# The last attention turn of an attention and token-mixer kernel: 18 tiles in place of 16, with the sums in two blocks

## Chip, cores and metric

The kernel runs on one core of a Trainium2 chip. The metric is device time in microseconds (us) for one execution, the median of several runs. A profile is one execution recorded by the hardware profiler; its times count from the first instruction. TensorE shows as PE in the profile (its weight loads as PEld), ScalarE as ACT, VectorE as DVE, GpSimd as POOL and SyncE as SP.

## What is computed

The reference runs two layers, each an attention and a mixer, both with a residual and a layer norm in front. There are 2,048 rows of 512 channels, 32 query heads of 16 channels, and one head of keys and values that all query heads share.

```python
def _A_ref(x, wq, wk, wv, wo):          # B, S, D = 1, 2048, 512; H = 32; Dh = 16
    q = (x @ wq).reshape(B, S, H, Dh).transpose(0, 2, 1, 3)
    k, v = x @ wk, x @ wv
    p = softmax(einsum("bhqd,bkd->bhqk", q, k) * Dh ** -0.5)
    o = einsum("bhqk,bkd->bhqd", p, v)
    return o.transpose(0, 2, 1, 3).reshape(B, S, H * Dh) @ wo
def _B_ref(x, w1, b1, w2, b2):          # mixes along the 2048 rows; F = 1792
    h = layernorm(x)
    u = gelu(einsum("bsd,sf->bdf", h, w1) + b1)
    return (einsum("bdf,fs->bds", u, w2) + b2).transpose(0, 2, 1)
x = x + _A_ref(layernorm(x), ...);  x = x + _B_ref(layernorm(x), ...)   # twice
```

## The kernel before, in words

**Tiles of attention.** Each layer's attention is cut into 32 groups, called cycles here: 4 blocks of 512 queries times 8 sets of 4 heads. A cycle has 32 tiles: 16 blocks of 128 keys times 2 pairs of heads. A layer has 1,024 tiles, counted by `scored` as they are begun. One tile passes through three engines:

- `scores` (line 915): two matmuls (line 921), one for each head of the pair, write 128 keys by 2 x 512 queries into a PSUM buffer called sc. There are three such buffers (`bank2`, lines 100 and 101, `bufs=3`), of two banks each, used in turn.
- ScalarE takes the exponential of the tile into an SBUF tile p (line 931). Either it reads PSUM itself, and the buffer is free when it ends, or the tile is *copied*: VectorE first copies sc into p (line 929), which frees the PSUM buffer, and ScalarE then works in place on p. In the profile the first kind is `p<-sc`, the second `p<-p`.
- `sums` (line 933): the matmuls of line 937 multiply p with the values and a column of ones, and add to the cycle's accumulator acc. The program issues two per tile; the trace holds four, each on 32 columns of the array, and those of one tile run side by side.

The tiles whose sums have not been issued are the list `pend`. `drain(count)` (line 942) issues the sums of the oldest ones. The p tiles come from a ring of 8 and a second ring of 4, of which every third tile takes one (`room`, line 908): twelve in all. The remaining two PSUM banks are single ones; cycles use them in turn for acc, and the bank that is not the current accumulator serves other products.

**Other work between the tiles.** When a pair of cycles is done, its sums are divided by the row sums on VectorE and multiplied with a part of the output weights: a *projection* (`project`, line 888; matmuls on line 898), into the spare single bank, whose result VectorE adds to x (`put`, line 903; the addition is on line 906). Mixer products that are known already are also placed between the tiles.

**Turns.** The order of all this is written by hand. `run` (line 997) asks `Mixer.turn` (line 1238) for the next turn, a tuple of numbers, and walks through it:

```python
if k > 0:                       # line 1041
    self.more(mix, k)           # begin k tiles; 10 + k: the last of the k is copied
elif k == 0:
    parts.pop(0)(self.spare())  # the next projection or half of a product
else:
    self.drain(-k)              # the sums of -k tiles; then a step of queued VectorE work
```

A turn is chosen when exactly `lag` tiles are pending. `lag` is 4 in the later part of a layer's attention and 2 in its last 16 tiles (line 1017). If the number differs, the turn is PLAIN, (2, -2), in which the number of sums is what brings the pending tiles back to `lag`, at most four. FOURS is the turn that is taken when more than three projections wait and 30 tiles of the last cycle are left to be summed. That is once in each layer, with 998 of 1,024 tiles begun (hence tile 998) and four pending. Its four projections belong to the second-to-last pair of cycles and have three matmuls each. Behind FOURS come plain turns to the end of the cycle. Then `rest` (line 1289) issues the sums of what is pending, and goes on with the mixer: its first product there is pu_e (line 1214).

**Around it.** Some 40 us ahead of the first FOURS another turn, QUAD (line 44), places four projections of six matmuls each and holds two blocks of six sums; the trace shows the second of them from 974.37 us.

Of the kernel before, what the change touches and what calls it, by code (L numbers as in the profile page):

```python
# [45 lines left out]
    2, -2, 13, 0, 13, -4, 13, 0, 13, -4, 3, -6, 13, 0, 13, 0, 3, -6, 13, -4, 3, -4,  # L46
)
ENTRY = (1, 0, 13, 0, 13, -4, 13, -4, 13, -4, 13, -4)
FOURS = (3, -4, 12, 0, 13, 0, -4, 3, -4, 12, 0, 13, -4, 0)
SHORT = (2, 0, 3, -4, 3, -4)  # L50
TINY = (2, 0, 2, -4)
PLAIN = (2, -2)
# [20 lines left out]
def kernel(  # L73
# [729 lines left out]
    class Attention:  # L803
# [193 lines left out]
        def run(self, mix, proj):  # L997
# [10 lines left out]
            while self.scored < total:  # L1008
# [31 lines left out]
                for k in turn:  # L1040
# [15 lines left out]
                    else:  # L1056
# [11 lines left out]
                        if self.pieces:  # L1068
                            self.pieces.pop(0)()
                        elif turn in (LONG, COPIED, ENTRY, DOUBLE, QUAD, QUAD_TO_FOUR, FOURS, WHOLE):  # L1070
                            room = 2.4 if turn in (COPIED, ENTRY, QUAD, QUAD_TO_FOUR) else 1.0
# [15 lines left out]
    class Mixer:  # L1087
# [150 lines left out]
        def turn(self, att):  # L1238
# [20 lines left out]
            if len(self.projections) > 3 and att.to_boundary() == 30 and att.scored > 2 * NKT * (NB * NG - 1):  # L1259
                return FOURS, [projection] * 4  # L1260
            if len(self.projections) > 1:
# [473 lines left out]
```

## Time and profile before

| | |
|---|---|
| median of 3 runs | 2511.52 us (2510.51 to 2512.19) |
| the profiled execution, its own time | 2511.45 us |
| its span, first to last instruction | 2509.7 us |
| mean granted TensorE clock | 0.998 |
| score matmuls, line 921 | 4,096, 683.4 us busy |
| sum matmuls, line 937 | 8,192, 999.7 us busy |
| exponentials from PSUM, line 931 | 1,441, 1404.4 us busy |
| exponentials of copied tiles, line 931 | 607, 659.4 us busy |
| copies by VectorE, line 929 | 607, 742.7 us busy |
| projection matmuls, line 898 | 360, 100.5 us busy |

A row of the timeline has the start, the length, the engine, the line of the kernel, the operation, the names of output and inputs, the shapes and how many instructions were merged into the row. In square brackets stands the idle time before it, and what ended it. Matmuls are pipelined: the next one starts before the last one's end, so a cost is read from start to next start. Rows of weight loads show idle time whenever a block of matmuls needs no new weights for a while; that alone is no wait of TensorE.

### The profile page before, as it was taken

What the parts mean: (1) busy time and instruction counts of PE and PEld (TensorE: products, weight loads), DVE (VectorE), ACT (ScalarE), POOL (GpSimd) and SP (SyncE); (2) the same over time, 40 slices, a digit from 0 to 9 for tenths busy, and PEclk for the clock granted to TensorE, in tenths of its full rate; (3) what the DMA queues carried; (4) which work ended last, traced back from release to release, by engine and by line L of the source; (5) the groups of instructions that cost most, each with busy time, mean ns of one, the idle gap of its engine ahead of it and who ended that gap; (6) DMA issues with size and microseconds to landing.
All of it is one profiled execution on the core that took longest, in us unless ns stands there. A gap on an engine that the chain in (4) does not pass through costs nothing. (4 is left out here: it accounts for less than half of the span.)

```text
span 2509.7 us, 41974 instructions
## 1 busy us (share of the span) xinstructions
PE 2493.1 (99%) x16170; PEld 1242.5 (50%) x16170; DVE 1554.8 (62%) x2462; ACT 2102.5 (84%) x2345; POOL 148.2 (6%) x235
## 2 busy tenths in 40 slices
PE   9999999999999999999999999999999999999999
PEld 6444344444444444588864343444444444445887
DVE  6565566667766776564445565666677667765522
ACT  6999999999999999653349999999999999995511
POOL 5000000000000000141000000000000000002200
PEclk9999999999999999999999999999999999999999
DMA  3221201111111111134414112111111111102343
GB/s 116 75 66 41 65 29 39 32 41 31 39 31 39 31 41 31 43 110 149 127 51 126 51 47 57 31 39 31 41 31 39 31 43 33 41 26 67 106 125 95
DMA packets 168679, 143.56 MB, mean 57 GB/s; under 512 B 17650, under 2 KB 132368, under 8 KB 167952
## 3 DMA queue, kind: packets, MB, share of 16 engines
q1 hardware_dynamic: 168464, 140.72, 18.9%
q8 instruction: 132, 2.16, 0.4%
q14 instruction: 83, 0.68, 0.1%
HBM read 97.67 MB, written 26.22 MB: 49 GB/s over the span
## 5 line engine op out<-in xcount | busy, mean ns | idle before, releaser
L931 ACT ACTIVATE p<-sc 128x1024 f32<-128x1024 f32 x1441 | 1404.4, 1050 | 63.5 <-PE sc L921 62.7
L929 DVE COPY p<-sc 128x1024 f32<-128x1024 f32 x607 | 742.7, 1224 | 525.2 <-PE sc L921 439.6
L937 PE MATMUL acc<-p,vaug 128*32 128x512 f32 x8192 | 999.7, 600 | 0.0
L921 PE MATMUL sc<-qs,kst 51*128 51x512 f32 x4096 | 683.4, 432 | 8.2 <-DVE kst L595 2.7
L931 ACT ACTIVATE p<-p 128x1024 f32<-128x1024 f32 x607 | 659.4, 1086 | 12.9 <-DVE p L929 8.2
L921 PEld LDWEIGHTS sc<-qs,kst 51*128 51x128 f32 x4096 | 338.8, 185 | 560.1 <-ACT p L931 390.2
L937 PEld LDWEIGHTS acc<-p,vaug 128*32 128x32 f32 x8192 | 218.6, 109 | 488.9 <-issue 474.6
L1467 PE MATMUL py<-u,w 128*128 128x512 f32 x1344 | 307.4, 390 | 0.0
L1467 PEld LDWEIGHTS py<-u,w 128*128 128x128 f32 x1344 | 251.9, 188 | 52.3
L1455 ACT CAST w<-w2r 128x896 fp32r<-128x896 f32 x64 | 60.3, 945 | 185.6 <-PE py L1467 177.8
L1214 PE MATMUL pu<-hb,w 128*128 128x512 f32 x792 | 209.6, 406 | 0.0
L1214 PEld LDWEIGHTS pu<-hb,w 128*128 128x128 f32 x792 | 140.9, 188 | 57.7 <-issue 31.8
L1201 POOL TENSOR_TENSOR w<-w1r,w 128x256 fp32r<-128x256 f32 x86 | 69.9, 821 | 1572.9 <-ACT w L1199 1571.8
L1456 DVE TENSOR_TENSOR w<-w2r,w 128x896 fp32r<-128x896 f32 x64 | 72.3, 1130 | 110.7 <-ACT w L1455 110.7
L857 DVE RECIPROCAL o<-o 128x128 f32<-128x128 f32 x120 | 113.3, 944 | 8.8 <-DMA o<-ev 8.8
L898 PE MATMUL po<-wo,hl 128*128 128x512 f32 x360 | 100.5, 412 | 0.1
L418 PE MATMUL pq<-hT,wq 128*128 128x512 f32 x312 | 81.4, 404 | 0.0
L898 PEld LDWEIGHTS po<-wo,hl 128*128 128x128 f32 x360 | 62.6, 188 | 34.0 <-issue 16.4
L839 DVE COPY ev<-acc 128x512 f32<-128x512 f32 x64 | 43.6, 682 | 56.0 <-PE acc L937 56.0
L1214 PE MATMUL pu_l<-hb,w 128*128 128x512 f32 x336 | 77.1, 389 | 0.0
L1473 DVE SCALAR_TENSOR_TENSOR x<-py,b2c,x 128x512 f32<-128x512 f32 x32 | 24.0, 750 | 81.6 <-PE py L1467 81.6
L1199 ACT CAST w<-w1r 128x256 fp32r<-128x256 f32 x86 | 34.3, 406 | 47.3 <-PE pu_l L1214 12.7
(191 smaller groups left out, 1181.9 us busy)
## 6 DMA issues: line engine op xcount, KB each, us to landing
w1r<-in_B_w_dram SPq DMA_DIRECT2D x224, 128.0 KB
w2r<-in_B_w_dram SPq DMA_DIRECT2D x64, 448.0 KB
qs<-qd SPq DMA_DIRECT2D x384, 64.0 KB
qd<-q SPq DMA_DIRECT2D x64, 256.0 KB
o<-ev SPq DMA_DIRECT2D x128, 128.0 KB
x<-in_A_x_dram SPq DMA_DIRECT2D x16, 256.0 KB
hd<-hT SPq DMA_DIRECT2D x2, 2048.0 KB
out_dram<-x SPq DMA_DIRECT2D x16, 256.0 KB
```

Of the source, the lines that this page charges most:

```text
L418: yield nc.tensor.matmul(out, a, c, start=(k == 0), stop=(k == len(terms) - 1))
L857: nc.vector.reciprocal(o[:, 1, c], o[:, 1, c])
L898: nc.tensor.matmul(po, a, c, start=(k == 0), stop=(k == 3 * len(parts) - 1))
L921: nc.tensor.matmul(sc[:, j, :], kst[kt // 4][rows, kt % 4 * P : (kt % 4 + 1) * P], qs[i % NQ][rows, j0 // 2, :], start=True, stop=True,)
L929: nc.vector.tensor_copy(pt, sc)
L931: nc.scalar.activation(pt, sc, AF.Exp, scale=0.25)
L937: nc.tensor.matmul(self.acc[i][c : c + 32, :], vaug[:, kt].rearrange("p d k -> p (d k)"), pt[:, j, :], start=(kt == 0), stop=(kt == NKT - ...
L1201: eng.tensor_tensor(w[:, 1], raw, f32(w[:, 0]), op=ALU.subtract)
L1214: nc.tensor.matmul(pu, a, c, start=(start and k == 0), stop=(stop and k == 5))
L1455: nc.scalar.copy(w[:, 0], raw)
L1456: nc.vector.tensor_tensor(w[:, 1], raw, f32(w[:, 0]), op=ALU.subtract)
L1467: nc.tensor.matmul(py, a, d, start=(c == 0 and f == 0 and k == 0), stop=(c == 1 and f == NFH - 1 and k == 2),)
```

## The change

One tuple is replaced; nothing else in the file differs.

```diff
-FOURS = (3, -4, 12, 0, 13, 0, -4, 3, -4, 12, 0, 13, -4, 0)
+FOURS = (-2, 13, 0, 13, 0, 13, -6, -4, 13, 0, 13, 0, 13, -2, -6)
```

Read with the rules above, the old turn begins 3 tiles, sums 4, begins 2 (the second copied), runs a projection, begins 3 (the third copied), runs a projection, sums 4, begins 3, sums 4, begins 2 (copied), a projection, begins 3 (copied), sums 4, a projection. That is 16 tiles begun, four of them copied, 16 summed and four projections. It leaves four tiles pending at 1,014 begun, where `lag` is 2, so a plain turn of two tiles and four sums follows.

The new turn sums 2, then begins three groups of 3 tiles (the third of each copied) with a projection after the first and the second group, sums 6 and 4, which makes ten in a row, begins three such groups again with the other two projections, and sums 2 and 6, eight in a row. That is 18 tiles begun, six of them copied, 20 summed and the same four projections. It leaves two tiles pending at 1,016 begun, which is where the old turn and its plain turn end.

## Prediction

> **What bounds the kernel now.** I read the page first, then the busy time by stretch, then the timeline of TensorE and ScalarE around the changed turn.
>
> ```profile
> PE 2493.1 (99%) x16170; PEld 1242.5 (50%) x16170; DVE 1554.8 (62%) x2462; ACT 2102.5 (84%) x2345; POOL 148.2 (6%) x235
> ```
>
> TensorE looks full over the whole span, but its ends are modelled, so a share says little about one turn. The turn runs once per layer, near 1013 us and near 2259 us. By stretch (columns: length, then busy time and count of PE, PEld, DVE, ACT, POOL, the granted clock, DMA):
>
> ```profile
> 1013.10:1031.90 18.80, 18.75 (x132) 6.95 (x128) 8.28 (x12) 17.97 (x20) 0.00 (x0) 1.00 0.04 15
> 1031.90:1041.00 9.10, 9.10 (x60) 2.50 (x56) 0.00 (x0) 7.77 (x10) 0.67 (x1) 1.00 0.01 3
> 2259.40:2278.20 18.80, 18.75 (x132) 6.94 (x128) 8.31 (x12) 17.96 (x20) 0.00 (x0) 1.00 0.04 15
> ```
>
> The two layers are alike to 0.03 us, so one is worked out and doubled. In the 18.80 us both TensorE (18.75) and ScalarE (17.97) are nearly full: the turn is balanced between the two. VectorE (8.28) and the DMAs (0.04) have room. TensorE's rows, from the turn's first scores to the scores that follow it:
>
> ```profile
> 1013.14 0.96 PE L921 MATMUL sc<-qs,kst 51*128 51x512 f32 x6
> 1014.03 1.92 PE L937 MATMUL acc<-p,vaug 128*32 128x512 f32 x16
> 1015.88 0.73 PE L921 MATMUL sc<-qs,kst 51*128 51x512 f32 x4
> 1016.55 0.97 PE L898 MATMUL po<-wo,hl 128*128 128x512 f32 x3
> 1017.45 1.10 PE L921 MATMUL sc<-qs,kst 51*128 51x512 f32 x6
> 1018.60 0.96 PE L898 MATMUL po<-wo,hl 128*128 128x512 f32 x3
> 1019.49 1.92 PE L937 MATMUL acc<-p,vaug 128*32 128x512 f32 x16
> 1021.35 0.97 PE L921 MATMUL sc<-qs,kst 51*128 51x512 f32 x6
> 1022.25 1.92 PE L937 MATMUL acc<-p,vaug 128*32 128x512 f32 x16
> 1024.10 0.73 PE L921 MATMUL sc<-qs,kst 51*128 51x512 f32 x4
> 1024.76 0.97 PE L898 MATMUL po<-wo,hl 128*128 128x512 f32 x3
> 1025.66 1.07 PE L921 MATMUL sc<-qs,kst 51*128 51x512 f32 x6
> 1026.65 1.92 PE L937 MATMUL acc<-p,vaug 128*32 128x512 f32 x16
> 1028.51 0.97 PE L898 MATMUL po<-wo,hl 128*128 128x512 f32 x3
> 1029.40 0.74 PE L921 MATMUL sc<-qs,kst 51*128 51x512 f32 x4
> 1030.07 1.92 PE L937 MATMUL acc<-p,vaug 128*32 128x512 f32 x16
> 1031.93 0.73 PE L921 MATMUL sc<-qs,kst 51*128 51x512 f32 x4
> ```
>
> The rows are the tuple itself: scores of 3 tiles, sums of 4, scores of 2, a projection, and so on; the last two before 1031.93 are the plain turn (2, -2), which scores two tiles and here sums four because four were pending. So the stretch of 18 tiles and 20 sums is before's turn of 16 tiles plus one plain turn. From start to next start: three tiles of scores 0.89, two 0.67 (1015.88 to 1016.55), four sums 1.85, a projection 0.90. ScalarE over the same stretch:
>
> ```profile
> 1013.02 1.08 ACT L931 ACTIVATE p<-p 128x1024 f32<-128x1024 f32 x1
> 1013.97 3.79 ACT L931 ACTIVATE p<-sc 128x1024 f32<-128x1024 f32 x4
> 1017.99 1.06 ACT L931 ACTIVATE p<-p 128x1024 f32<-128x1024 f32 x1 [0.23 <-DVE p L929]
> 1018.95 1.92 ACT L931 ACTIVATE p<-sc 128x1024 f32<-128x1024 f32 x2
> 1020.76 1.06 ACT L931 ACTIVATE p<-p 128x1024 f32<-128x1024 f32 x1
> ...
> 1032.53 7.44 ACT L931 ACTIVATE p<-sc 128x1024 f32<-128x1024 f32 x8 [0.58 <-PE sc L921]
> ```
>
> An exponential from PSUM takes 0.91 of ScalarE (two from 1018.95 to 1020.76), one of a copied tile 0.95 (1013.02 to 1013.97). ScalarE runs almost without a break while sums come four at a time; the rows show 0.23 and 0.58 idle. The row that carries the end is the last: eight exponentials back to back, then this.
>
> ```profile
> 1039.10 0.14 PEld L937 LDWEIGHTS acc<-p,vaug 128*32 128x32 f32 x4 [0.77 <-ACT p L931]
> ...
> 1041.00 3.06 PE L1214 MATMUL pu_e<-hb,w 128*128 128x512 f32 x12
> ```
>
> After the stretch the last sums wait for ScalarE (0.77), and the mixer's rest follows them at once. So whatever delays the exponential of 1032.53 delays the layer's end by as much; nothing behind it absorbs that.
>
> **The change, part by part.** *Work.* Before: 16 tiles and 16 sums, then a plain turn's 2 tiles and 4 sums. After: 18 tiles and 20 sums, leaving the same two pending. Same scores, sums and projections, no DMA, no step moved past a queue (no queued division step is left: VectorE has only copies and additions here). Six tiles are copied by VectorE in place of four: two exponentials at 0.95 for 0.91, 0.08 us of ScalarE, and 2 x 1.22 on VectorE, which has room. What changes is the order: sums of 2, then three groups of 3 scores with 2 projections between, sums of 10, the same groups again, sums of 8.
>
> *TensorE alone.* Before by pieces: 4 x 0.89 + 3 x 0.67 scores, 5 x 1.85 sums, 4 x 0.90 projections: 18.42, against 18.79 in the rows (1013.14 to 1031.93), so 0.37 is waits. A block of six sums is in the trace some 40 us earlier, behind groups of two, three and three tiles with two projections, much as here; ScalarE beside it:
>
> ```profile
> 974.37 2.78 PE L937 MATMUL acc<-p,vaug 128*32 128x512 f32 x24
> 977.08 0.50 PE L921 MATMUL sc<-qs,kst 51*128 51x512 f32 x2
> ```
>
> ```profile
> 973.60 1.06 ACT L931 ACTIVATE p<-p 128x1024 f32<-128x1024 f32 x1
> 974.55 1.94 ACT L931 ACTIVATE p<-sc 128x1024 f32<-128x1024 f32 x2
> 976.35 1.07 ACT L931 ACTIVATE p<-p 128x1024 f32<-128x1024 f32 x1
> 977.71 1.02 ACT L931 ACTIVATE p<-sc 128x1024 f32<-128x1024 f32 x1 [0.28 <-PE sc L921]
> ```
>
> Six take 2.71, two more than four for 0.86: 0.43 a sum and 0.13 once per block. Ten then take 4.43, eight 3.57; no row has such blocks. The other end is a block that scales whole, 10 x 1.85 / 4 = 4.63 and 3.70; I take the first, which two rows give, and keep 0.33 a layer for the range. A two joined to the four ahead of it costs 0.86. After by pieces: 6 x 0.89 + 0.86 + 4.43 + 3.57 + 4 x 0.90 = 17.80. TensorE has 0.62 less to do per layer, from fewer, longer blocks.
>
> The Trainium skill, "TensorEngine Tiling (Array Packing)", section Key Properties, says that a change of tiling mode drains TensorE; by that rule fewer blocks are a gain. The rows agree so far as each block costs more than its tiles; its result is the rival of TensorE's work below.
>
> *ScalarE during a long block.* This is what I hold to decide. While TensorE sums, it makes no scores, and ScalarE lives on what lies ready: three PSUM buffers and a copied tile. The six-sum rows show it: sums begin at 974.37, ScalarE has work until 977.42, next scores start at 977.08 and their exponential at 977.71, 0.6 after. Six sums already cost 0.28 of idle ScalarE. Four more cost 4 x 0.43 = 1.7 on top.
>
> *The walk.* Zero is 1013.14, the end of the sums ahead; t0 is the first tile. Two rows give the releases:
>
> ```profile
> 1016.73 1.22 DVE L929 COPY p<-sc 128x1024 f32<-128x1024 f32 x1 [2.65 <-PE sc L921]
> 1017.87 0.68 DVE L906 TENSOR_TENSOR x<-x,po 128x512 f32<-128x512 f32 x1
> ```
>
> ```profile
> 1017.81 0.38 PEld L921 LDWEIGHTS sc<-qs,kst 51*128 51x128 f32 x4 [0.18 <-ACT p L931]
> ```
>
> Scores reuse a PSUM buffer three tiles on, 0.05 after its reader ends (1017.76 to 1017.81); a pair's copy starts 0.85 after the pair's scores (1015.88 to 1016.73) and takes 1.22.
> - Two sums first: scores of t0 at 0.86, exponential at 1.46. Before it was at 0.83 (1013.97): 0.63 lost.
> - Exponentials: t0 1.46, t1 2.37, t2 (copied) 3.28, t3 4.23, t4 5.14, t5 (copied) 6.05, t6 7.00, t7 7.91, t8 (copied) 8.82; ScalarE is free at 9.77.
> - Scores between: t0 to t2 at 0.86, projection 1.75, t3 at 2.65; t4 waits for t1's exponential (2.37 + 1.02) and starts at 3.44, t5 behind it; second projection 4.10; t6 after t3's exponential, 5.30; t7 after t4's, 6.21, t8 behind it. Each exponential finds its scores ready.
> - Sums of ten start at 6.21 + 0.67 = 6.88 and end at 11.31; exponential of t9 at 11.91. ScalarE idles 2.14.
> - Same again, 10.45 later: sums of eight start at 17.33, end at 20.90; the first of the last eight exponentials at 21.50.
>
> Before it stood at 19.39 (1032.53). The change costs 2.11 us a layer: ScalarE gains idle time of 0.63, 2.14 and about 1.3 and loses that of before. The first projection's addition starts when t2's copy ends (about 3.1) and takes 0.68: done at 3.8, before the second projection at 4.10. The last eight tiles run as before, shifted.
>
> *The sum.* 2 x 2.11 = 4.2 us on the profiled execution, 2511.45 (span 2509.7 and 1.75 around it), 0.07 under the median of 2511.52: 2515.6. If blocks scale whole: 2 x 0.33 more, 2516.3.
>
> **Rivals.**
> - *TensorE's work decides.* ScalarE's idle time turns out covered, and the turn falls to TensorE's pieces: 18.79 to 17.80, at most 0.99 a layer, 2509.5. For it: TensorE is busy 18.75 of 18.80. Against it: the 0.28 idle of a mere six sums. Even this is under 0.2% of gain, so nothing here can be faster by more.
> - *VectorE falls behind in the score groups.* Three copies and two additions are 3 x 1.22 + 2 x 0.68 = 5.0 us in the 6.0 of nine tiles. t5's copy ends at 3.44 + 0.85 + 1.22 = 5.51 and t8's scores need its buffer at 6.55, so it decides once a copy is over 1.0 us late. With both additions ahead of it, 1.36: 0.36 in four groups, 1.4 us, to 2517.0, slower by over 0.2%. Against it: program order puts one addition ahead of that copy, not two.
> - *The clock drops.* TensorE now waits for PSUM inside the score groups, 0.5 us or so at t4 and at t7. At half the clock the blocks of ten and eight would take 8.0 longer a layer, 16 in all: 2531.6. It decides if waits longer than those of before come. Against it: the stretch from 1031.90 holds waits of 0.77 at a granted 1.00.
>
> The Trainium skill, "TensorE: Matmul & The Clock Gate", section "A second HAM failure mode: psum-queue depth-cycling", tells of micro-idles between groups that made the clock swing; no run here shows that so far.
>
> **How the numbers follow.** 0.2%, about what a measurement of this kernel can tell from no change, is 5.0 us, from 2506.5 to 2516.5. Idle ScalarE 0.71, which lies within it (2515.6 to 2516.3); TensorE's work 0.05, within; VectorE 0.17 and the clock 0.04, slower; 0.03 for a gain that no row shows. So faster 0.03, same 0.76, slower 0.21. The range starts at 2513.8: the forecast less the opening's 0.63 in both layers and 0.3 a layer of backlog I may have missed. It ends at 2518.0: VectorE's case with blocks that scale whole. Outside lie TensorE's case, the clock's and the unseen gain, 0.12, and some of the rest.
>
> **What would show it.** In the profile after, both turns hold blocks of 40 and 32 sum matmuls, the first from about 6.9 us after 1013.14 and some 4.4 long; ScalarE shows idle gaps of about 2.1 and 1.3 us ended by scores; the row of eight exponentials starts at about 1034.6 in place of 1032.53, and 4.2 later than before in the second layer. VectorE's copies of scores number 4 more over the span. I am wrong if ScalarE stays busy through the ten sums, if the rows of eight start no later than before, or if the time moves elsewhere.

## Result and the profile after

| | before | after |
|---|---|---|
| median of 17 runs | 2512.64 us (2509.75 to 2513.82) | 2516.71 us (2514.22 to 2519.39) |
| span of the profiled execution | 2509.7 | 2515.0 |

The ratio is 1.0018, with a 95% interval from 1.0011 to 1.0024. The median is 4.1 us longer where 4.2 was forecast, 0.16% of the time and so within the 0.2% that was named as no change. (Of 17 runs the median of before is 1.1 us above that of the first three, and the forecast of 2515.6 misses the new median by as much. That 4.1 and 4.2 agree to 0.1 is therefore partly luck; what bears the forecast out is the two turns below.)

The profile after shows where the 4 us lie. TensorE's rows of the first layer's turn, as before from the timeline:

```profile
1012.15 2.78 PE L937 MATMUL acc<-p,vaug 128*32 128x512 f32 x24
1014.87 0.97 PE L921 MATMUL sc<-qs,kst 51*128 51x512 f32 x6
1015.76 0.96 PE L898 MATMUL po<-wo,hl 128*128 128x512 f32 x3
1016.66 0.51 PE L921 MATMUL sc<-qs,kst 51*128 51x512 f32 x2
1017.46 0.73 PE L921 MATMUL sc<-qs,kst 51*128 51x512 f32 x4 [0.30 <-ACT p L931]
1018.12 0.97 PE L898 MATMUL po<-wo,hl 128*128 128x512 f32 x3
1019.32 0.50 PE L921 MATMUL sc<-qs,kst 51*128 51x512 f32 x2 [0.23 <-ACT p L931]
1020.23 0.73 PE L921 MATMUL sc<-qs,kst 51*128 51x512 f32 x4 [0.41 <-ACT p L931]
1020.90 4.50 PE L937 MATMUL acc<-p,vaug 128*32 128x512 f32 x40
1025.33 0.96 PE L921 MATMUL sc<-qs,kst 51*128 51x512 f32 x6
...
1031.36 3.64 PE L937 MATMUL acc<-p,vaug 128*32 128x512 f32 x32
1034.93 0.74 PE L921 MATMUL sc<-qs,kst 51*128 51x512 f32 x4
```

The first row holds the four sums ahead of the turn and its two. The walk's zero, the end of the four, is 1012.15 + 1.85 = 1014.00 here. (This execution had reached the turn 0.87 us later than the one of before, which has nothing to do with the change.) Then come groups of scores that wait for ScalarE to free PSUM (0.30, 0.23, 0.41), and one row of 40 matmuls: the ten sums, 4.43 from start to next start. ScalarE, from the tile ahead of the turn to the row of eight:

```profile
1013.88 1.07 ACT L931 ACTIVATE p<-p 128x1024 f32<-128x1024 f32 x1
1015.47 1.94 ACT L931 ACTIVATE p<-sc 128x1024 f32<-128x1024 f32 x2 [0.51 <-PE sc L921]
1017.29 1.06 ACT L931 ACTIVATE p<-p 128x1024 f32<-128x1024 f32 x1
1018.24 1.94 ACT L931 ACTIVATE p<-sc 128x1024 f32<-128x1024 f32 x2
1020.05 1.08 ACT L931 ACTIVATE p<-p 128x1024 f32<-128x1024 f32 x1
1021.00 1.96 ACT L931 ACTIVATE p<-sc 128x1024 f32<-128x1024 f32 x2
1022.80 1.09 ACT L931 ACTIVATE p<-p 128x1024 f32<-128x1024 f32 x1
1025.93 1.94 ACT L931 ACTIVATE p<-sc 128x1024 f32<-128x1024 f32 x2 [2.03 <-PE sc L921]
...
1033.27 1.10 ACT L931 ACTIVATE p<-p 128x1024 f32<-128x1024 f32 x1
1035.54 7.54 ACT L931 ACTIVATE p<-sc 128x1024 f32<-128x1024 f32 x8 [1.18 <-PE sc L921]
```

Three gaps, each ended by scores: 0.51 after the opening sums, 2.03 behind the ten, 1.18 behind the eight. The row of eight starts at 1035.54, which is 21.54 after zero; before it was 19.39. That is 2.15 in this layer, and in the second layer it is 21.52, 2.13 more than before. So 4.3 us of the difference of the two spans (5.3) lie in the two turns. Of the rest, 0.9 had come up ahead of the first turn; there, as in the other stretches outside the turns, the two programs are the same.

The page's groups, for the counts, first before and then after:

```profile
L931 ACT ACTIVATE p<-sc 128x1024 f32<-128x1024 f32 x1441 | 1404.4, 1050 | 63.5 <-PE sc L921 62.7
L929 DVE COPY p<-sc 128x1024 f32<-128x1024 f32 x607 | 742.7, 1224 | 525.2 <-PE sc L921 439.6
```

```profile
L931 ACT ACTIVATE p<-sc 128x1024 f32<-128x1024 f32 x1437 | 1401.0, 1050 | 69.5 <-PE sc L921 68.9
L929 DVE COPY p<-sc 128x1024 f32<-128x1024 f32 x611 | 747.9, 1224 | 527.1 <-PE sc L921 444.0
```

Four more copies (611 for 607), and ScalarE's idle time ahead of exponentials from PSUM 69.5 in place of 63.5.

### The profile page after: what moved, and what is told of

Same layout as the page of the kernel before. It is cut to its first block, busy times and chain, and to the rows that moved or that the text cites. A ratio compares the mean times of both kernels' runs of the same rounds, so it can differ in the third digit from the quotient of the medians.

```text
span 2515.0 us, 41978 instructions
## 1 busy us (share of the span) xinstructions
PE 2493.4 (99%) x16170; PEld 1242.4 (49%) x16170; DVE 1559.0 (62%) x2466; ACT 2102.4 (84%) x2345; POOL 148.4 (6%) x235
## 3 DMA queue, kind: packets, MB, share of 16 engines
q1 hardware_dynamic: 168464, 140.72, 19.2%
## 5 line engine op out<-in xcount | busy, mean ns | idle before, releaser
L931 ACT ACTIVATE p<-sc 128x1024 f32<-128x1024 f32 x1437 | 1401.0, 1050 | 69.5 <-PE sc L921 68.9
```

The costliest lines, as they stand in the source:

```text
L931: nc.scalar.activation(pt, sc, AF.Exp, scale=0.25)
```

## Experiments

All are read in the same way: the stretch from zero to the start of ScalarE's row of eight. Zero is also 0.12 after the start of the last copied tile's exponential ahead of the turn (1013.02 before, 1013.88 after). The stretch repeats to a few hundredths between layers, while the total time of one execution moves by some us for other reasons (last section), so single times are not compared. (Some views end inside the row of eight, which then shows with fewer exponentials, x4 for instance; its start is what counts.) The theory is that ScalarE runs out of ready tiles in the long blocks of sums; the main rival, that TensorE's own work decides, by which fewer blocks would gain.

### The opening two sums moved

The edit is against the changed kernel:

```diff
-FOURS = (-2, 13, 0, 13, 0, 13, -6, -4, 13, 0, 13, 0, 13, -2, -6)
+FOURS = (13, -2, 0, 13, 0, 13, -6, -4, 13, 0, 13, 0, 13, -2, -6)
```

> The changed turn with its opening two sums moved behind the first three tiles of scores: (13, -2, 0, 13, 0, 13, -6, -4, ...). Read: the stretch from the end of the four sums ahead of the turn to the start of the row of eight exponentials; 19.39 us in the kernel before, 21.54 in the changed one. Theory (ScalarE starves): only the opening's idle time of ScalarE, 0.5 to 0.6 us, goes; the 2.0 in the ten sums and the 1.2 in the eight stay; the stretch is 20.9. Rival (TensorE's work decides): one block more, so 21.7, slower than the changed kernel.

ScalarE's rows of this kernel:

```profile
1012.84 1.08 ACT L931 ACTIVATE p<-p 128x1024 f32<-128x1024 f32 x1
1013.79 1.95 ACT L931 ACTIVATE p<-sc 128x1024 f32<-128x1024 f32 x2
...
1024.26 1.94 ACT L931 ACTIVATE p<-sc 128x1024 f32<-128x1024 f32 x2 [2.03 <-PE sc L921]
...
1033.85 3.87 ACT L931 ACTIVATE p<-sc 128x1024 f32<-128x1024 f32 x4 [1.17 <-PE sc L921]
```

The first gap is gone and the other two stand unchanged. The stretch is 1033.85 - 1012.96 = 20.89, in both layers: 0.65 shorter than the changed kernel, although TensorE has one block more. That is the number of the theory; the rival had 21.7.

### Three tiles put into the ten sums

```diff
-FOURS = (-2, 13, 0, 13, 0, 13, -6, -4, 13, 0, 13, 0, 13, -2, -6)
+FOURS = (-2, 13, 0, 13, 0, 13, -6, 13, -4, 0, 13, 0, 13, -2, -6)
```

> The changed turn with three tiles of scores put between the six and the four of the ten sums, taken from behind it: (-2, 13, 0, 13, 0, 13, -6, 13, -4, 0, 13, 0, 13, -2, -6). Theory (ScalarE starves in long blocks): the idle time of 2.03 us in the ten sums falls to about 0.4 behind the six, but the shorter groups behind it leave less lying ready, so that the stretch is about 20.7, 0.8 shorter than the changed kernel's 21.54. Rival (TensorE's work decides): the same sums in one block more, 21.7.

```profile
1022.35 1.94 ACT L931 ACTIVATE p<-sc 128x1024 f32<-128x1024 f32 x2 [0.31 <-PE sc L921]
1024.17 1.06 ACT L931 ACTIVATE p<-p 128x1024 f32<-128x1024 f32 x1
1026.00 1.94 ACT L931 ACTIVATE p<-sc 128x1024 f32<-128x1024 f32 x2 [0.77 <-PE sc L921]
...
1032.83 4.79 ACT L931 ACTIVATE p<-sc 128x1024 f32<-128x1024 f32 x5 [1.18 <-PE sc L921]
```

Behind six sums ScalarE idles 0.31, as it did behind six in the kernel before (0.28). A gap of 0.77 is new: three tiles do not last for four sums and the projection behind them. The stretch is 20.67 in both layers against 21.54, again with one block more. So the 2.03 belonged to the length of the block.

### Half the exponential, in both orders

The same edit in the kernel before and in the changed one:

```diff
+            half = 998 < self.scored <= 1016
             if copied:
                 nc.vector.tensor_copy(pt, sc)
                 sc = pt
+            elif half:
+                nc.gpsimd.memset(pt[:, :, QB // 2 :], 1.0)
+            if half:
+                pt, sc = pt[:, :, : QB // 2], sc[:, :, : QB // 2]
             nc.scalar.activation(pt, sc, AF.Exp, scale=0.25)
```

> The order before, but in the 18 tiles the exponential covers only the first 256 of each head's 512 columns; GpSimd fills the other half with ones where the tile is not copied (copied tiles keep the scores there), so this part of the softmax is left out. Theory (TensorE bounds the order before): ScalarE's work nearly halves and the stretch hardly moves from 19.39, 19.2 to 19.4. Rival (ScalarE bounds it): it falls by a us or more.

> The changed order with the same half exponentials in the 18 tiles (the rest of those columns filled with ones by GpSimd or left as copied scores, so this part of the softmax is left out). Theory (the loss is ScalarE's time that the long sum blocks cannot cover): with ScalarE's work halved the long blocks no longer cost anything, and the stretch falls from 21.54 to about 19.0, under the order before with the same halves (19.3). Rival (the long blocks cost TensorE itself something, or the order's waits do): it stays above 20.5.

The sums ahead of the turn and the scores behind it on TensorE, and the start of the row of eight on ScalarE, first in the order before, then in the changed order. (Zero is 1.85 after the first row's start.)

```profile
1012.02 1.92 PE L942 MATMUL acc<-p,vaug 128*32 128x512 f32 x16
...
1032.89 0.73 PE L921 MATMUL sc<-qs,kst 51*128 51x512 f32 x4
1033.51 1.02 ACT L936 ACTIVATE p<-sc 128x1024 f32<-128x1024 f32 x1 [1.45 <-PE sc L921]
```

```profile
1010.10 2.78 PE L942 MATMUL acc<-p,vaug 128*32 128x512 f32 x24
...
1030.27 0.73 PE L921 MATMUL sc<-qs,kst 51*128 51x512 f32 x4
```

```profile
1022.59 1.09 ACT L936 ACTIVATE p<-sc 128x512 f32<-128x512 f32 x2 [2.96 <-PE sc L921]
...
1030.89 3.85 ACT L936 ACTIVATE p<-sc 128x1024 f32<-128x1024 f32 x4 [2.12 <-PE sc L921]
```

The order before: 1032.89 - 1013.87 = 19.02, and 19.64 to the row of eight. That is not shorter than 19.39 but 0.25 longer, and so outside the 19.2 to 19.4 that was expected. A row of VectorE ahead of the turn shows why:

```profile
1010.60 1.50 DVE L1204 CAST w<-w1r 128x256 fp32r<-128x256 f32 x1
```

This cast takes 0.28 in the kernel before (mean of 138). Here it runs beside GpSimd's fills, which the experiment brought in, and the copies queued behind it come late: the turn's first three tiles of scores take 1.10 (1013.88 to 1014.98) in place of 0.89, which is 0.21 of the 0.25. So ScalarE's halved work gained nothing in this order, as the theory says, but the experiment's own cost blurs it by 0.2.

The changed order: 1030.27 - 1011.95 = 18.32, against 20.93 with whole exponentials; to the row of eight 18.94 where 19.0 was expected. Its gaps on ScalarE are longer than ever (2.96 behind the ten), and cost nothing. With ScalarE's work halved the sign turns: the changed order is 0.70 shorter than the order before. About 0.2 of that is what the fills cost the order before, so 0.5 is left, a little less than the 0.62 by which its pieces are fewer (18.42 to 17.80); its first three tiles of scores take 0.89 as usual. The rival's gain is real, and it was reached here, where ScalarE no longer sets the pace.

### No copies by VectorE

```diff
-FOURS = (-2, 13, 0, 13, 0, 13, -6, -4, 13, 0, 13, 0, 13, -2, -6)
+FOURS = (-2, 3, 0, 3, 0, 3, -6, -4, 3, 0, 3, 0, 3, -2, -6)
```

> The changed turn without VectorE's copies: all 18 tiles go from PSUM by ScalarE alone. Theory (what ScalarE has lying ready decides): a copied tile is a fourth one lying ready beside the three in PSUM; without it ScalarE has about one tile less at the start of each long block, 0.5 to 0.9 more idle time in each, and the stretch is 22.5 to 23.0 in place of 21.54. Rival (VectorE falls behind in the score groups): without the copies the groups run freer, 21.5 or less.

```profile
1012.54 1.07 ACT L931 ACTIVATE p<-p 128x1024 f32<-128x1024 f32 x1
1014.12 8.36 ACT L931 ACTIVATE p<-sc 128x1024 f32<-128x1024 f32 x9 [0.50 <-PE sc L921]
1025.24 8.36 ACT L931 ACTIVATE p<-sc 128x1024 f32<-128x1024 f32 x9 [2.77 <-PE sc L921]
1035.50 1.94 ACT L931 ACTIVATE p<-sc 128x1024 f32<-128x1024 f32 x2 [1.91 <-PE sc L921]
```

The gaps grow by 0.74 and 0.73, the stretch to 1035.50 - 1012.66 = 22.84. So a copied tile is worth 0.7 of cover in each long block, and VectorE did not hold the groups up.

### Long blocks in the ten QUAD turns

This edit and the last one are against the kernel before:

```diff
-QUAD = (13, -4, 13, 0, 3, -6, 13, 0, 13, -4, 3, -4, 12, 0, 13, 0, 13, -6, 13, -4, 13, -4)
+QUAD = (13, 13, 0, 3, -4, -6, 13, 0, 13, 3, -4, -4, 12, 0, 13, 0, 13, -6, 13, 13, -4, -4)
```

> The kernel before with its ten QUAD turns in the manner of the change: the sums in blocks of 10, 8, 6 and 8 where they were 4, 6, 4, 4, 6, 4 and 4, the same 32 tiles, projections and copies but one order: (13, 13, 0, 3, -4, -6, 13, 0, 13, 3, -4, -4, 12, 0, 13, 0, 13, -6, 13, 13, -4, -4). Theory (ScalarE starves in long blocks): the same walk gives about 4.1 us more in each QUAD, 41 us in ten, 2553, and ScalarE's idle time ended by scores grows by as much. Rival (TensorE's work decides): three blocks fewer in each QUAD, about 1 us less, 10 us faster in all, 2502.

2573.71 against 2511.78 in the same series, ratio 1.0251 (1.0232 to 1.0269): 62 us longer. The direction is the theory's, and ScalarE's idle time ended by scores grew from 62.7 to 112.6; the size is half as much again as the 41 expected. The trace, of the fastest of its four runs (2565.64), shows two parts. The five QUADs without a drop of the clock cost 4.2 to 4.7 more each, where 4.1 was walked. But in the other five the granted clock fell eight times in all. Two of the drops (columns as in the prediction, PEclk behind POOL):

```profile
587.60:591.00 3.40, 2.01 (x11) 1.10 (x10) 1.86 (x3) 3.40 (x5) 0.00 (x0) 1.00 0.22 77
591.00:594.40 3.40, 3.40 (x15) 1.75 (x17) 1.39 (x2) 3.22 (x5) 0.00 (x0) 0.50 0.00 0
...
874.30:877.70 3.40, 2.25 (x16) 0.97 (x12) 1.75 (x2) 3.13 (x4) 0.00 (x0) 1.00 0.30 81
877.70:881.10 3.40, 3.40 (x18) 0.78 (x20) 2.80 (x4) 3.05 (x4) 0.00 (x0) 0.50 0.01 2
```

A stretch of 3.4 us with TensorE busy for 2.01 or 2.25 of it is followed by one at half the clock. The five QUADs that hold drops cost 6.2 to 8.8 more each; over 4.2 each that is about 14 for eight drops, 1.7 a drop. So of the 54 us between the two spans some 14 are drops and some 43 the QUADs themselves, less about 2 by which this execution was faster outside of them. The three runs that took 8 to 14 us longer had mean clocks of 0.988 to 0.991 in place of 0.994, which fits more drops, but they were not profiled. So the third rival, the clock, appears here, with scores that wait longer than in the changed turn: TensorE waited 0.97 and 0.42 in the first of these stretches.

### Before, with its second projection behind the sums

```diff
-FOURS = (3, -4, 12, 0, 13, 0, -4, 3, -4, 12, 0, 13, -4, 0)
+FOURS = (3, -4, 12, 0, 13, -4, 0, 3, -4, 12, 0, 13, -4, 0)
```

> The order before with one exchange, its second projection behind the four sums and not ahead of them: (3, -4, 12, 0, 13, -4, 0, 3, -4, 12, 0, 13, -4, 0). Theory (before, TensorE bounds the turn with a few small waits): the second projection no longer waits for VectorE's addition of the first, and the stretch is 19.1 in place of 19.39, 0.3 a layer, 0.5 us in all, less than the times can tell. Rival (ScalarE bounds the order before): no shorter.

```profile
1019.01 1.92 PE L937 MATMUL acc<-p,vaug 128*32 128x512 f32 x16
1020.87 0.96 PE L898 MATMUL po<-wo,hl 128*128 128x512 f32 x3
```

The projection now starts 1.86 after the sums, with no wait for VectorE's addition. The stretch is 19.26, 0.13 shorter than before in each layer, half of what was expected: the three tiles of scores ahead of the sums still take 1.03 (1017.98 to 1019.01) in place of 0.89, because one of them waits for an exponential, as it did before (1017.81 there). Only the 0.12 that the addition had cost is gone. The time, 2511.32 against 2511.78, ratio 0.9997 (0.9987 to 1.0007), cannot tell the two apart. No order tried here beats the kernel before by anything that the times show.

## Why the prediction was right, step by step

- **The opening.** t0's scores at 0.87 and its exponential at 1.47, forecast 0.86 and 1.46. That it costs a gap of its own is shown by the first experiment.
- **Six, ten and eight sums.** 4.43 and 3.57 were forecast from 0.43 a sum and 0.13 a block, and 4.43 and 3.57 are in the rows. The other bound, blocks that scale whole (4.63), is not borne out.
- **The groups between.** t3 at 2.66, t4 3.46, second projection 4.12, t6 5.32, t7 6.23, sums of ten 6.90; forecast 2.65, 3.44, 4.10, 5.30, 6.21, 6.88. The waits end with exponentials on ScalarE, as the walk has it; that they are those of t1, t3 and t4 is read from their times.
- **ScalarE's gaps.** 0.51, 2.03 and 1.18 for 0.63, 2.14 and 1.3. The start of each later exponential is as forecast. The gaps are about 0.1 shorter because exponentials overlap: a row ends some 0.1 after the next could have started, and the walk counted from start to start.
- **The sum.** 2.15 and 2.13 a layer for 2.11. That nothing behind it absorbs the delay: in the second layer the time from the row of eight to the span's end is 230.8 before and 230.9 after.
- **The range.** By the terms that the prediction names, its ends come to 2513.7 and 2517.7, where it says 2513.8 and 2518.0. The measured 2516.71 lies inside either way.
- **TensorE's work**, the first rival, fell by the gap of 2.03; the half exponentials show a condition under which it would have held.
- **VectorE**, the second, was not late. Its rows after:

```profile
1017.08 0.68 DVE L906 TENSOR_TENSOR x<-x,po 128x512 f32<-128x512 f32 x1
1018.30 1.23 DVE L929 COPY p<-sc 128x1024 f32<-128x1024 f32 x1 [0.54 <-PE sc L921]
```

t5's copy ends at 1019.53. The row with the scores of t7 and of t8, which needs t5's buffer, starts at 1020.23 and waits for ScalarE until then, so the copy had at least 0.7 to spare.
- **The clock**, the third, stayed at 1.00 through the turn. A stretch of the profile after, in the groups ahead of the ten sums:

```profile
1018.70:1022.10 3.40, 2.76 (x20) 0.90 (x22) 2.45 (x3) 3.40 (x5) 0.00 (x0) 1.00 0.00 0
```

TensorE is busy for 2.76 of 3.40 there; counted on the grid that this execution's drops keep (last section), 2.76 is the least in the turn, while from another start, 1016.90, 3.4 us hold only 2.46. In the QUAD experiment the drops came behind stretches with 2.01 to 2.43, and many stretches with 2.25 or more had none. So the turn may have come near a drop. The outcome was forecast, but the argument was weak: it compared the length of single waits (0.77 without a drop), and in the QUAD experiment no wait longer than 0.73 stood in some of the stretches ahead of a drop. The price of this rival was also wrong. It took both long blocks at half the clock, 8.0 a layer; the drops seen last 3.4 us and cost about 1.7 each.

## What to carry to other kernels

Where one engine feeds another through a few buffers, ask what lies ready for the second engine when a block of the feeder's other work begins: in this kernel that set how long the block could be at no cost. Here three PSUM tiles and a copied one cover about five sums, and each sum beyond costs its full 0.43. Fewer and longer blocks on the feeder paid only where the other engine had slack, so ask first which engine the stretch belongs to. This turn of 20 us could be walked by hand from a dozen rows to within 0.05 us, far finer than the times can tell.

## What the runs showed that was not expected

**The clock dropped after stretches in which TensorE waited much, but not after all of them.** In the QUAD experiment it fell to half for 3.4 us, eight times within the turns, behind stretches of 3.41 us with 2.01 to 2.43 us of TensorE work. The starts of all nine drops of this execution (one lies between the layers) are whole multiples of 3.413 us apart (591.0, 604.7, 621.7, 877.7 and so on to 2150.9), so the stretches are counted on that grid. No single wait in the eight stretches was longer than 1.12. Thirteen other stretches of the QUADs with 2.25 to 2.43 had no drop behind them, so the busy share alone does not decide. Where the waits lie in the stretch seems to matter: one tile of scores between a wait of about 0.74 and one of 0.42 started 1.56 to 1.89 us into the stretch in the five that a drop followed, and 0.75 to 1.36 into it in five that none followed. What the rule is stays open. The Trainium skill, "TensorE: Matmul & The Clock Gate", section "A second HAM failure mode: psum-queue depth-cycling", tells of a kernel whose clock swings because of micro-idles between groups of matmuls. The QUAD experiment agrees so far as the eight drops, at about 1.7 us each, came without any wait over 1.12.

**The spread between executions goes with the clock.** Of the 17 runs after, the six with a mean granted clock of 0.999 took 2514.2 to 2514.8, the eight at 0.997 took 2517.5 to 2519.4. Before, runs at 0.998 and 0.999 took 2510.1 to 2512.3 in the last series, those at 0.996 and 0.997 2514.2 to 2514.7. The traces show where the clock is lost: in the profiled executions before and after it is at half for one such stretch near 50 us and for two from about 1297 us, in that of the first experiment for one at each place, all far from the changed turn (the last 2 us left aside). Why one execution loses more than another stays open.

**GpSimd's fills can hold VectorE up.** In the half-exponential experiments a cast of 0.28 took 1.50 and 1.47 beside the fills in the two layers of the order before, and 0.57 and 1.47 in those of the changed order; VectorE's copies out of PSUM kept their 1.2. Nothing in the kernel's own turn runs on GpSimd.
